# A second-layer loop with the quarter sums on another engine, one-bank accumulators and a second value buffer (Trainium2, one core)

## The chip, the cores and the metric

The kernel runs on one core of a Trainium2 chip. The metric is device time in microseconds (us): the median over several executions.

## The reference, cut to what matters

Attention feeds a gated layer, and that feeds a second layer. Only the second layer is touched by the change, apart from a few operations that are fitted into the end of the first.

```python
# attention: B=4, H=8, S=576, D=64, scores below max - tau are dropped -> x: 2304 tokens x 512
# layer 1: x1 = (sigmoid(x @ w_gate) * (x @ w_val)) @ w_out        (hidden 1536)
# layer 2: hidden 2048
h = x1 @ w_in
g = np.where(h >= 1, h, np.where(h <= -1, 0.0, (h + 1) ** 2 / 4.0))
return (g @ w_out).astype(np.float32)
```

## The kernel before, in words

**Numbers.** A float32 operand is held as a high part (rounded to fp32r) and a low part (value minus high part). Each product is three matmuls: high·high, high·low, low·high. ScalarE makes each high part by a copy, VectorE makes the low part by a subtraction.

**Stages.** Attention takes the time to about 290 us, layer 1 to about 747 us, layer 2 the rest. Layer 2 goes over the 2304 tokens in three passes of 768 (`NPASS`), and in each pass over 8 pairs of hidden blocks (`NQ`), 24 pairs in all, numbered from 0. Pairs 0, 8 and 16 are the first of a pass.

**A pair** (`pair`, L658). The up projection of a pair is a 2×2 block product done with seven products, P0 to P6 (`product`, L609), instead of eight. Each is six matmuls of 384 columns into one of two one-bank PSUM tiles `pu`. The token side of the seven products is built from sums and differences of the four quarters of the pass's input (two halves of the features, two halves of the tokens): `x_sums` (L565, four operations, L575 to L578) makes them once per pass, and `x_split` (L581: ScalarE L584, VectorE L585) splits seven blocks of them into high and low. The weight side is `tsum`, loaded per pair, and `w_split` (L587: ScalarE L591, VectorE L592) splits it: blocks of 512, 256 and 1024 columns.

Between the products small operations free the PSUM tiles and put the results together: after P0 ScalarE copies the tile to `s1` (L688); after P1 VectorE adds `c[0]`'s first token half (L677); after P2 ScalarE copies `u2` (L699); after P3, P4, P5, P6 VectorE adds again (all group under the line of the helper, L677). So P2 waits for the `s1` copy, P3 for the first add, P4 for `u2`, P5 and P6 for adds. The two results `c[0]` and `c[1]` (768 columns each) go through `activate` (L624): ScalarE does relu and square into `sqs` (L627, L628), VectorE a max and min (L630, here STT for its name SCALAR_TENSOR_TENSOR), ScalarE the high part `hh` (L631), VectorE the low part `hl` (L633). `out_split` (L598) splits the down weights `wout` (ScalarE L601, VectorE L602).

**The down projection** of a pair (`down_pair`, L715, matmul L723) is 36 matmuls of 512 columns into six accumulators of a PSUM bank each, held as three two-bank tiles `w`. It stands on TensorE behind the products of the next pair: products of pair q, down of pair q−1, products of pair q+1. It needs `hh`, `hl` and both `wout` parts of pair q−1. TensorE's order is fixed.

**Order of the other work.** Splits and the steps of `activate` are put on a list by `due`, with a date, a first and a last slot and a cost; `fill` (twice in a pair: behind P1, and at the pair's end) takes from it what fits the room. That sets the order in which ScalarE's and VectorE's in-order queues get their instructions. The SP queue issues the loads of a pair (`load_sums`, `load_pair`) and the stores of the pass before in one order.

**Ends of passes.** Layer 1's last token block is copied out of PSUM by `finish` (L746; VectorE L750, ScalarE L752), alternately. At the end of a pass `store` (L754, L764 and L766) copies the accumulators out the same way and stores them; this is behind the first down projection of the next pass. `x_sums(t + 1)` stands in pair 6 and 14 (j = NQ−2) in the code and runs on GpSimd, and `x_sums(0)` stands in layer 1's last steps. Behind the last pair, the tail does blocks 0 to 3 of `down_pair(22)` first, then interleaves the rest with the last pair's.

Of the kernel before, what the change touches and what calls it, by code (L numbers as in the profile page):

```python
# [10 lines left out]
F32 = mybir.dt.float32  # L11
# [18 lines left out]
def kernel(  # L30
# [17 lines left out]
    nc = tc.nc  # L48
# [23 lines left out]
    dram = ctx.enter_context(pool("dram", 2, space=DRAM))  # L72
    ps_w = ctx.enter_context(pool("ps_w", 1, space=PSUM))

# [124 lines left out]
    def attention():  # L199
# [4 lines left out]
        ps_o = ctx.enter_context(ExitStack())  # L204
        banks = ps_o.enter_context(pool("ps_o", 1, space=PSUM))
        left, av = (banks.tile([P, 512], F32, name=n) for n in ("left", "av"))
# [248 lines left out]
    def ffn(att):  # L455


        with ExitStack() as st:
# [108 lines left out]
            def x_sums(t):  # L567

                a11, a12, a21, a22 = (
                    xall[:, k * HK : (k + 1) * HK, t * T + n * HT :][:, :, :HT] for n in range(2) for k in range(2)  # L570
                )
                flat = [ssum[:, i] for i in range(2)]
                s1, s2, s4 = (x.rearrange("p (k t) -> p k t", k=HK) for x in (*flat, early_raw[0][:, : BX // 2]))
                op = nc.gpsimd.tensor_tensor
                op(s1, a21, a22, op=ALU.add)  # L575
                op(s2, s1, a11, op=ALU.subtract)
                op(s4, a12, s2, op=ALU.subtract)
                op(a21, a11, a21, op=ALU.subtract)  # L578
# [44 lines left out]

            def activate(i, c, h):  # L624

                r = sqs[:, i]
                nc.scalar.activation(r, c, AF.Relu, scale=0.5, bias=half)  # L627
                nc.scalar.activation(r, r, AF.Square)  # L628
                yield
                nc.vector.scalar_tensor_tensor(c, c, 1.0, r, op0=ALU.max, op1=ALU.min)  # L630
                nc.scalar.activation(h[0], c, AF.Copy)  # L631
                yield
                nc.vector.tensor_tensor(h[1], c, f32(h[0]), op=ALU.subtract)  # L633
                yield
# [7 lines left out]

            def due(at, release, last, cost, what):
                waiting.append((at, len(waiting), release, last, cost, what))
                waiting.sort(key=lambda x: x[:2])

            def fill(slot, room):
                while True:
                    now = [x for x in waiting if x[2] <= slot and (x[4] <= room or x[3] <= slot)]
                    if not now:  # L650
                        return
                    x = now[0]
                    waiting.remove(x)
                    room -= x[4]
                    x[5]()

            def due_x(t):
                q = t * NQ  # L658
                for i in range(7):
                    first = 3 * (q - 1) + max(1, min(i, 2))  # L660
                    last = 3 * q - 1 if i < 2 else 3 * q + 1
                    due(start(q) + i - 1, first, last, 0.93, lambda i=i: x_split(t, i))

            def due_w(q):
                for i, (p, first, last, cost) in enumerate(
                    ((0, 3 * q - 2, 3 * q - 1, 0.67), (6, 3 * q - 1, 3 * q + 1, 0.4), (2, 3 * q - 1, 3 * q + 1, 1.2))
                ):
                    due(start(q) + p - 1, first, last, cost, lambda i=i: w_split(q, i))

            def pair(q):  # L670

                t, j = divmod(q, NQ)
                ps = [ps_a.tile([P, 512], F32, tag=f"a{i}", name="pu")[:, :HT] for i in range(2)]
                c = [vals[:, 0], (vals[:, 1], rbs, early_raw[1])[q % 3][:, :T]]
                s1, u2 = (hp_.tile([P, HT], F32, tag="act", name="act") for _ in range(2))
# [15 lines left out]
                fill(3 * q + 1, 1.5)  # L691
# [38 lines left out]
            def at(y, a, b):  # L730
                return y[a // 1024].rearrange("p a b -> p (a b)")[:, a % 1024 : a % 1024 + b - a]

# [21 lines left out]
            def store(t, y, i):  # L754
                x = xall[:, :, t * T : (t + 1) * T]
                o = x[:, i, :DM].unsqueeze(1) if i < KD else x[:, 2 * (i - KD) : 2 * (i - KD) + 2, DM:]
                src = y[i % 3][:, i // 3].rearrange("p (a b) -> p a b", a=o.shape[1])
                r0 = t * T + i * P
# [55 lines left out]
            cp = cv("cp", 1, side="right")  # L814
            ps_a = sb("ps_a", 1, space=PSUM)
            for i in range(2):
# [10 lines left out]
            run(more, second)  # L827
            wides.extend(taken)
            NS = len(order)
            for s in range(NS):  # L830
# [5 lines left out]
                if s == NS - 3:  # L836
# [17 lines left out]
                if s == NS - 1:  # L854
# [3 lines left out]
                    due_w(0)  # L858
                    fill(-1, 4.4)
                _, t, f = order[s - 1]  # L860
                if s > 0:
                    if f == 0:
                        y = [wide() for _ in range(3)]
                    down(t, f, y)
                    if f == NF[0] - 1:
                        finish(t, y)
            for q in range(NPASS * NQ):
# [67 lines left out]
```

## Time and profile before

| | |
|---|---|
| median of 3 runs | 1162.38 us (1161.56 to 1163.65) |
| profiled execution, its own time | 1163.97 us |
| its span in the trace | 1161.9 us |
| mean granted TensorE clock, share of full | 0.988 |
| TensorE matmul busy | 1118.1 us, 96% of the span |
| VectorE busy | 848.2 us, 73% |
| ScalarE busy | 619.4 us, 53% |
| GpSimd busy | 166.5 us, 14% |

The profile's page comes from one execution. Engines are PE (TensorE matmul), PEld (its weight loads), DVE (VectorE), ACT (ScalarE), POOL (GpSimd) and SP (the queue that issues DMAs). A row of a timeline gives start, duration, engine, line, operation, output and inputs, shapes and count; in brackets stands how long the engine was idle before it, and what released it.

### The profile page before, as it was taken

What the parts mean: (1) busy time and instruction counts of PE and PEld (TensorE: products, weight loads), DVE (VectorE), ACT (ScalarE), POOL (GpSimd) and SP (SyncE); (2) the same over time, 40 slices, a digit from 0 to 9 for tenths busy, and PEclk for the clock granted to TensorE, in tenths of its full rate; (3) what the DMA queues carried; (4) which work ended last, traced back from release to release, by engine and by line L of the source; (5) the groups of instructions that cost most, each with busy time, mean ns of one, the idle gap of its engine ahead of it and who ended that gap; (6) DMA issues with size and microseconds to landing.
All of it is one profiled execution on the core that took longest, in us unless ns stands there. A gap on an engine that the chain in (4) does not pass through costs nothing.

```text
span 1161.9 us, 17313 instructions
## 1 busy us (share of the span) xinstructions
PE 1118.1 (96%) x6372; PEld 949.1 (82%) x6372; DVE 848.2 (73%) x1472; ACT 619.4 (53%) x1048; POOL 166.5 (14%) x327
## 2 busy tenths in 40 slices
PE   8999999999899999999999999989998999999998
PEld 5655655656799999999999999878987888878886
DVE  7888888887699998776786672656667666766663
ACT  5777777777444435333343322455565565655653
POOL 3444544454100000000000030110004000000000
PEclk9999999999899999999999999989998999999999
DMA  4323223222556555555455343122331433233301
GB/s 128 90 76 97 72 73 81 70 55 66 210 165 207 199 192 207 181 168 182 149 181 189 111 142 113 55 73 92 108 109 55 163 109 109 90 125 112 109 19 54
DMA packets 65140, 139.08 MB, mean 120 GB/s; under 512 B 9616, under 2 KB 35872, under 8 KB 65056
## 3 DMA queue, kind: packets, MB, share of 16 engines
q1 hardware_dynamic: 64912, 137.98, 35.9%
q8 instruction: 50, 0.82, 0.3%
q14 instruction: 34, 0.28, 0.1%
q10 hardware_dynamic: 144, 0.00, 0.0%
HBM read 111.15 MB, written 26.81 MB: 119 GB/s over the span
## 4 chain that ended last, share of the span: by engine, by line
PE 80%; DVE 11%; ACT 4%; issue 3%; DMA 1%; SPq 0%; POOL 0%; DVEq 0%; POOLq 0%; ACTq 0%
PE w L723 13%; PE pu L619 13%; PE w L741 12%; PE pgv L484 8%; PE pgv L485 8%; PE pgv L486 8%; PE av L318 6%; PE w L294 5%; PE w L251 5%; DVE s L260 2%; PE w L247 2%; DVE p L280 1%; DVE win L592 1%; DVE vals L630 1%; DVE high L164 1%
## 5 line engine op out<-in xcount | busy, mean ns | idle before, releaser
L484 PE MATMUL pgv<-xflat,win 128*128 128x384 f32 x560 | 189.1, 338 | 5.7 <-ACT act L540 4.1
L485 PE MATMUL pgv<-xflat,win 128*128 128x384 f32 x560 | 188.6, 337 | 0.1
L486 PE MATMUL pgv<-xflat,win 128*128 128x384 f32 x560 | 188.5, 337 | 0.0
L723 PE MATMUL w<-wout,hh 128*128 128x512 f32 x576 | 184.3, 394 | 0.6 <-ACT hh L631 0.6
L741 PE MATMUL w<-hh,wout 128*128 128x512 f32 (+1 forms) x576 | 147.2, 338 | 0.0
L260 DVE TENSOR_SCALAR_CACHE_REDUCE s<-w,nscale 128x576 f32<-128x576 f32 x144 | 112.7, 817 | 33.2 <-PE w L251 23.4
L723 PEld LDWEIGHTS w<-wout,hh 128*128 128x128 f32 x576 | 108.2, 188 | 25.4 <-ACT hh L631 1.1
L619 PE MATMUL pu<-xflat,win 128*128 128x384 f32 x576 | 112.8, 351 | 8.9 <-ACT act L699 4.8
L619 PEld LDWEIGHTS pu<-xflat,win 128*128 128x128 f32 x576 | 105.8, 198 | 12.5 <-ACT act L699 6.6
L723 PE MATMUL w<-wout,hl 128*128 128x512 f32 x288 | 113.7, 395 | 0.5 <-DVE hl L633 0.5
L484 PEld LDWEIGHTS pgv<-xflat,win 128*128 128x128 f32 x560 | 106.2, 190 | 8.5 <-ACT act L540 5.0
L280 DVE SCALAR_TENSOR_TENSOR p<-s,mx,ex 128x576 f32<-128x576 f32 x144 | 112.0, 811 | 0.5 <-POOL lt L287 0.5
L544 DVE TENSOR_TENSOR act<-pgv,act 128x384 f32<-128x384 f32 x70 | 38.9, 555 | 98.4 <-PE pgv L486 97.1
L272 ACT ACTIVATE ex<-s,mx 128x576 f32<-128x576 f32 x144 | 104.8, 775 | 6.5 <-DVE s L260 6.1
L741 PEld LDWEIGHTS w<-hh,wout 128*128 128x128 f32 x576 | 98.6, 189 | 11.4
L485 PEld LDWEIGHTS pgv<-xflat,win 128*128 128x128 f32 x560 | 106.2, 190 | 2.0 <-DVE xflat L476 0.4
L486 PEld LDWEIGHTS pgv<-xflat,win 128*128 128x128 f32 x560 | 106.1, 190 | 0.0
L540 ACT ACTIVATE act<-pgv 128x384 f32<-128x384 f32 x70 | 34.2, 489 | 133.3 <-PE pgv L486 133.1
L545 ACT ACTIVATE hh<-act 128x384 fp32r<-128x384 f32 x72 | 37.9, 526 | 119.7 <-DVE act L544 119.7
L741 PE MATMUL w<-hl,wout 128*128 128x512 f32 (+1 forms) x288 | 97.5, 338 | 0.0
L294 PEld LDWEIGHTS w<-ident,p 128*128 128x128 f32 x576 | 62.8, 141 | 41.6 <-ACT ex L272 36.6
L294 PE MATMUL w<-ident,p 128*128 128x128 f32 x576 | 79.4, 278 | 13.6 <-DVE p L280 10.5
(132 smaller groups left out, 1942.8 us busy)
## 6 DMA issues: line engine op xcount, KB each, us to landing
wmore<-saved SPq DMA_DIRECT2D x32, 512.0 KB
words<-in_moe_w_out_dram SPq DMA_DIRECT2D x26, 512.0 KB
tsum<-tsaved SPq DMA_DIRECT2D x24, 512.0 KB
wmore<-saved SPq DMA_DIRECT2D x15, 768.0 KB
words<-in_moe_w_in_dram SPq DMA_DIRECT2D x16, 512.0 KB
saved<-w SPq DMA_DIRECT2D x16, 512.0 KB
w<-saved SPq DMA_DIRECT2D x16, 512.0 KB
w<-saved SPq DMA_DIRECT2D x9, 768.0 KB
```

The costliest lines, as they stand in the source:

```text
L251: nc.tensor.matmul(w[:, s, :HS], t[es, 0, u * P : u * P + P], t[es, 1, c], start=True, stop=True)
L260: nc.vector.tensor_scalar(t[:, e], w[:, :, :HS], nscale, None, op0=ALU.mult, op1=ALU.min, accum_out=mx[:, 0, e : e + 1])
L272: nc.scalar.activation(ex[:, e], t[:, e], AF.Exp, scale=-1.0, bias=mx[:, 0, e : e + 1])
L280: nc.vector.scalar_tensor_tensor(pr[:, e], t[:, e].rearrange("p a b -> p (a b)"), mx[:, 1, e : e + 1], ex[:, e].rearrange("p a b -> p (a b ...
L294: nc.tensor.transpose(wt[:, e, cs], pr[:, e, cs], ident)
L318: nc.tensor.matmul(av[e * D : e * D + D, :n], vs[p % 3][:, e, c], rt[r][:, e, c] if c < nf else rl[r], start=c == 0, stop=c == nf,)
L484: nc.tensor.matmul(ps, ih[:, i, kk], xh[:, kk, c], start=(kk == 0), stop=False)
L485: nc.tensor.matmul(ps, ih[:, i, kk], xl[:, kk, c], start=False, stop=False)
L486: nc.tensor.matmul(ps, il[:, i, kk], xh[:, kk, c], start=False, stop=(kk == KD - 1))
L619: nc.tensor.matmul(ps[bank], l[:, k], r[:, k], start=bool(new) and k == m == 0, stop=k == HK - 1 and m == 2, skip_group_check=True,)
L723: nc.tensor.matmul(y[b % 3][:, b // 3], l[:, ts_], r, start=first and m == 0, stop=last and m == 2)
L741: nc.tensor.matmul(at(y, a, b), l[:, ds_], r[:, c], start=new and m == 0, stop=last and m == 2, skip_group_check=True,)
```

## The change

1. The four operations of `x_sums` move from GpSimd to VectorE. For the first pass they are worked into a step of layer 1. For the next passes they are put on the list in pair 4 (12), at dates from 8 units past the start of pair 5 (13) on, and `x_sums` in pair 6 (14) goes.
2. The six accumulators become six tiles `y_0` to `y_5` of one bank. `finish` gives even banks to VectorE and odd ones to ScalarE; before, it alternated piece by piece.
3. `c[0]` alternates between `sqs[:, 1]` and `vals[:, 0]`; before it was always `vals[:, 0]`. Both halves' squares go through the one buffer `sqs[:, 0]`; before, each had its own.
4. `due` and `fill` count ScalarE's time next to VectorE's, with other costs and other last slots.
5. In the tail the blocks 0 to 4 of `down_pair(22)` come first, and the last pair's second relu is dated earlier.

```diff
-                op = nc.gpsimd.tensor_tensor
+                op = nc.vector.tensor_tensor
                 op(s1, a21, a22, op=ALU.add)
+                yield
...
-            def activate(i, c, h):
-
-                r = sqs[:, i]
+            def activate(c, r, h):
+
                 nc.scalar.activation(r, c, AF.Relu, scale=0.5, bias=half)
...
-            def fill(slot, room):
+            def fill(slot, room, act):
                 while True:
-                    now = [x for x in waiting if x[2] <= slot and (x[4] <= room or x[3] <= slot)]
+                    now = [x for x in waiting if x[2] <= slot and (x[4] <= room and x[5] <= act or x[3] <= slot)]
...
                     room -= x[4]
-                    x[5]()
+                    act -= x[5]
+                    x[6]()
...
-                c = [vals[:, 0], (vals[:, 1], rbs, early_raw[1])[q % 3][:, :T]]
+                c = [(sqs[:, 1], vals[:, 0])[q % 2], (vals[:, 1], rbs, early_raw[1])[q % 3][:, :T]]
...
+                if j == NQ - 4 and t + 1 < NPASS:
+                    g = x_sums(t + 1)
+                    for i in range(4):
+                        due(start(q + 1) + 8 + 10 * i, 3 * q, 3 * (q + 3) - 1, 0.92, 0, lambda g=g: next(g))
...
-                    due(at - 1.8 + 0.3 * i, 3 * q, 3 * q + 2, 0.67, lambda i=i: out_split(q, i))
+                    due(at - 1.8 + 0.3 * i, 3 * q, 3 * q + 4, 0.6, 0.5, lambda i=i: out_split(q, i))
...
-                if j == NQ - 2 and t + 1 < NPASS:
-                    x_sums(t + 1)
...
-                    g = activate(i, c[i], h[i])
-                    for when, cost in (((-4, 0), (-1.9, 0.92), (-1.7, 0.92)), ((-1.6, 0), (1, 0.92), (2.5, 0.92)))[i]:
-                        last = 3 * q + 2 if i == 0 else 3 * q + 5
-                        due(at + when, 3 * q + 2, last, cost, lambda g=g: next(g))
-                fill(3 * q + 2, LEN(q) - (8 if j == 0 else 6))
+                    g = activate(c[i], vals[:, 1] if i and not more else sqs[:, 0], h[i])
+                    when = ((-4, -1.9, -1.7), (-1.6 if more else -3, 1, 2.5))[i]
+                    for w, d, a in zip(when, (0, 0.85, 0.85), (1.6, 0.72, 0)):
+                        due(at + w, 3 * q + 2, 3 * q + 5, d, a, lambda g=g: next(g))
+                drain = 2 if j == 0 else 0
+                fill(3 * q + 2, LEN(q) - 6 - drain, LEN(q) - 6 - drain)
...
-                                y[b % 3][:, b // 3], l[:, ts_], r, start=first and m == 0, stop=last and m == 2
+                                y[b], l[:, ts_], r, start=first and m == 0, stop=last and m == 2
...
-                    if i % 2 == 0:
+                    if a // 512 % 2 == 0:
                         nc.vector.tensor_copy(dst, at(y, a, b))
...
-                    x_sums(0)
+                    work = x_sums(0)
...
+                        yp = sb("ps_y", 1, space=PSUM)
+                        y = [yp.tile([P, 512], F32, name=f"y_{i}") for i in range(T // P)]
...
-            for b in (range(4), (4,), (5,)):
+            for b in (range(5), (5,)):
                 down_pair(q - 1, y, b)
```

TensorE's order is the same but for the tail, SP's is the same, and GpSimd loses its twelve sums. On ScalarE and VectorE the order moves at the starts and ends of passes and in pairs 4 and 12; in a regular pair it stays. Line numbers of the changed kernel are up to 9 higher.

ScalarE in pair 0, between the end of layer 1 and pair 1 (`xall<-w` and `xall<-y` are `finish`'s copies; `act<-pu` is `s1` or `u2`). Before:

```order
L631 ACTIVATE hh<-vals 128x768
L601 ACTIVATE wout_89<-wmore 128x512
L601 ACTIVATE wout_3013<-wmore 128x512
L752 ACTIVATE xall<-w_128 128x256
L752 ACTIVATE xall<-w_127 128x512
L752 ACTIVATE xall<-w_126 128x256
L752 ACTIVATE xall<-w_126 128x512
L688 ACTIVATE act<-pu 128x384
L627 ACTIVATE sqs<-vals,half 128x768
L628 ACTIVATE sqs<-sqs 128x768
L631 ACTIVATE hh<-vals 128x768
L699 ACTIVATE act<-pu 128x384
```

After:

```order
L760 ACTIVATE xall<-y_3229 128x256 x2
L760 ACTIVATE xall<-y_3231 128x512
L760 ACTIVATE xall<-y_3233 128x512
L697 ACTIVATE act<-pu 128x384
L606 ACTIVATE wout_89<-wmore 128x512
L635 ACTIVATE hh<-sqs 128x768
L606 ACTIVATE wout_3013<-wmore 128x512
L706 ACTIVATE act<-pu 128x384
```

The first pair's `hh` and both `wout` copies stood ahead of `finish`'s copies and of pair 1's `s1`; now they stand behind `s1`, and between it and `u2`. The second relu and square moved from ahead of `u2` to behind it.

ScalarE in pair 8, the first of the second pass. Before:

```order
L584 ACTIVATE xflat<-raw_86 128x768
L631 ACTIVATE hh<-vals 128x768
L601 ACTIVATE wout_6533<-wmore 128x512
L688 ACTIVATE act<-pu 128x384
L627 ACTIVATE sqs<-rb,half 128x768
L628 ACTIVATE sqs<-sqs 128x768
L631 ACTIVATE hh<-rb 128x768
L699 ACTIVATE act<-pu 128x384
L591 ACTIVATE win_88<-wmore 128x512
```

After:

```order
L589 ACTIVATE xflat<-raw_86 128x768
L635 ACTIVATE hh<-vals 128x768
L697 ACTIVATE act<-pu 128x384
L606 ACTIVATE wout_6543<-wmore 128x512
L706 ACTIVATE act<-pu 128x384
L631 ACTIVATE sqs<-rb,half 128x768
L632 ACTIVATE sqs<-sqs 128x768
L635 ACTIVATE hh<-rb 128x768
L596 ACTIVATE win_88<-wmore 128x512
```

The `u2` copy (the second `act<-pu`) moved ahead of the relu, square and `hh` of pair 7's second half.

VectorE at the end of pair 4 and the start of pair 5. Before:

```order
L630 SCALAR_TENSOR_TENSOR vals<-vals,sqs 128x768
L633 TENSOR_TENSOR hl<-vals,hh 128x768
L602 TENSOR_TENSOR wout_3013<-wmore,wout_3013 128x512
L630 SCALAR_TENSOR_TENSOR rb<-rb,sqs 128x768
L633 TENSOR_TENSOR hl<-rb,hh 128x768
L677 TENSOR_TENSOR vals<-pu,act 128x384
```

After:

```order
L634 SCALAR_TENSOR_TENSOR sqs<-sqs 128x768
L637 TENSOR_TENSOR hl<-sqs,hh 128x768
L607 TENSOR_TENSOR wout_3013<-wmore,wout_3013 128x512
L576 TENSOR_TENSOR ssum<-xall 128x768
L634 SCALAR_TENSOR_TENSOR rb<-rb,sqs 128x768
L637 TENSOR_TENSOR hl<-rb,hh 128x768
L578 TENSOR_TENSOR ssum<-ssum,xall 128x768
L580 TENSOR_TENSOR raw_86<-xall,ssum 128x768
L682 TENSOR_TENSOR vals<-pu,act 128x384
```

Three of the four sums stand in the pair's last stretch, two of them between the last `hl` and the add of pair 5 that P3 waits for; the fourth comes one pair later.

## Rows read from the trace of the kernel before

**Rows 1.** Page, part 1: busy time of the engines.
```profile
PE 1118.1 (96%) x6372; PEld 949.1 (82%) x6372; DVE 848.2 (73%) x1472; ACT 619.4 (53%) x1048; POOL 166.5 (14%) x327
```
**Rows 2.** Chain of waits (start, us, what): layer 1's last matmuls, first products of five pairs.
```profile
743.44 4.19 PE w L741 x24
...
802.89 7.33 PE pu L619 x42
...
865.63 7.34 PE pu L619 x42
...
938.55 7.33 PE pu L619 x42
...
1001.59 7.34 PE pu L619 x42
...
1069.41 7.33 PE pu L619 x42
```
**Rows 3.** Timeline of PE at the starts of the three passes.
```profile
755.08 3.13 PE L619 MATMUL pu<-xflat,win 128*128 128x384 f32 x12 [1.94 <-DVE high L677]
...
768.96 0.44 PE L619 MATMUL pu<-xmore,win 128*128 128x384 f32 x1 [3.66 <-ACT act L688]
...
887.28 1.32 PE L619 MATMUL pu<-xflat,win 128*128 128x384 f32 x6 [2.16 <-DVE vals L677]
...
890.59 0.69 PE L619 MATMUL pu<-xflat,win 128*128 128x384 f32 x1 [1.98 <-ACT act L699]
...
1023.71 0.62 PE L619 MATMUL pu<-xflat,win 128*128 128x384 f32 x2 [1.47 <-ACT act L699]
```
**Rows 4.** Windows: stretch, length, PE, PEld, DVE, ACT, POOL busy, granted clock, DMA share, GB/s.
```profile
755.00:766.00 11.00, 10.23 (x48) 9.22 (x48) 7.40 (x12) 4.95 (x8) 3.34 (x2) 0.84 0.25 70
770.00:777.00 7.00, 6.37 (x21) 5.86 (x20) 2.08 (x3) 2.51 (x5) 0.00 (x0) 0.51 0.00 0
873.00:885.00 12.00, 11.66 (x54) 9.52 (x52) 11.09 (x13) 8.45 (x13) 5.82 (x2) 1.00 0.24 87
891.00:897.00 6.00, 6.00 (x21) 5.91 (x21) 1.60 (x4) 2.51 (x4) 0.00 (x0) 0.55 0.00 0
1020.00:1024.00 4.00, 2.53 (x14) 2.04 (x14) 2.14 (x4) 2.94 (x5) 0.00 (x0) 1.00 0.40 131
```
**Rows 5.** Timeline of VectorE in pair 8.
```profile
884.46 2.31 DVE L602 TENSOR_TENSOR wout<-wmore,wout 128x512 fp32r<-128x512 f32 x1
...
887.15 2.13 DVE L630 SCALAR_TENSOR_TENSOR rb<-rb,sqs 128x768 f32<-128x768 f32 x1
```
**Rows 6.** Timeline of GpSimd in pair 8.
```profile
883.79 2.42 POOL L576 TENSOR_TENSOR ssum<-ssum,xall 128x768 f32<-128x768 f32 x1
```
**Rows 7.** Timeline of VectorE around the start of pair 7, a regular pair.
```profile
863.68 0.69 DVE L602 TENSOR_TENSOR wout<-wmore,wout 128x512 fp32r<-128x512 f32 x1 [1.27 <-ACT wout L601]
864.29 0.95 DVE L630 SCALAR_TENSOR_TENSOR vals<-vals,sqs 128x768 f32<-128x768 f32 x1
...
867.82 0.56 DVE L677 TENSOR_TENSOR vals<-pu,act 128x384 f32<-128x384 f32 x1 [0.70 <-PE pu L619]
```
**Rows 8.** ScalarE's groups, 930 to 1000 us, by form: busy, mean ns, idle before, releaser.
```profile
L628 ACT ACTIVATE sqs<-sqs 128x768 f32<-128x768 f32 x10 | 8.5, 848 | 0.3
L627 ACT ACTIVATE sqs<-vals,half 128x768 f32<-128x768 f32 x6 | 5.5, 920 | 0.0
L591 ACT ACTIVATE win<-tsum 128x1024 fp32r<-128x1024 f32 x5 | 5.3, 1062 | 12.8 <-PE pu L619 12.8
L631 ACT ACTIVATE hh<-vals 128x768 fp32r<-128x768 f32 x6 | 5.1, 847 | 8.4 <-DVE vals L630 8.4
L601 ACT ACTIVATE wout<-wmore 128x512 fp32r<-128x512 f32 x5 | 3.1, 614 | 0.0
...
L688 ACT ACTIVATE act<-pu 128x384 f32<-128x384 f32 x4 | 2.0, 492 | 2.6 <-PE pu L619 2.6
```
**Rows 9.** Page, part 5: a group of the down projection's matmuls.
```profile
L723 PE MATMUL w<-wout,hh 128*128 128x512 f32 x576 | 184.3, 394 | 0.6 <-ACT hh L631 0.6
```

More of the change, by code (lines that the diff above doesn't have):

```diff
@@ L72 @@
     dram = ctx.enter_context(pool("dram", 2, space=DRAM))
-    ps_w = ctx.enter_context(pool("ps_w", 1, space=PSUM))
+    ps_st = ctx.enter_context(ExitStack())
+    ps_w = ps_st.enter_context(pool("ps_w", 1, space=PSUM))
     ident = const.tile([P, P], F32, name="ident")
@@ L204, in attention @@
         ps_o = ctx.enter_context(ExitStack())
-        banks = ps_o.enter_context(pool("ps_o", 1, space=PSUM))
+        banks = ps_o.enter_context(pool("ps_o", 1, space=PSUM, side="right"))
         left, av = (banks.tile([P, 512], F32, name=n) for n in ("left", "av"))
@@ L573, in x_sums @@
                 s1, s2, s4 = (x.rearrange("p (k t) -> p k t", k=HK) for x in (*flat, early_raw[0][:, : BX // 2]))
-                op = nc.gpsimd.tensor_tensor
+                op = nc.vector.tensor_tensor
                 op(s1, a21, a22, op=ALU.add)
+                yield
                 op(s2, s1, a11, op=ALU.subtract)
+                yield
                 op(s4, a12, s2, op=ALU.subtract)
+                yield
                 op(a21, a11, a21, op=ALU.subtract)
                 xops[t] = (a11, a12, s2, a21, s1, a22, s4)
+                yield
             def x_split(t, i):
@@ L641, in ffn, with due @@
             start = lambda q: sum(LEN(i) for i in range(q))
-            def due(at, release, last, cost, what):
-                waiting.append((at, len(waiting), release, last, cost, what))
+            def due(at, release, last, cost, act, what):
+                waiting.append((at, len(waiting), release, last, cost, act, what))
                 waiting.sort(key=lambda x: x[:2])
-            def fill(slot, room):
+            def fill(slot, room, act):
                 while True:
-                    now = [x for x in waiting if x[2] <= slot and (x[4] <= room or x[3] <= slot)]
+                    now = [x for x in waiting if x[2] <= slot and (x[4] <= room and x[5] <= act or x[3] <= slot)]
                     if not now:
@@ L661, in due_x @@
                     last = 3 * q - 1 if i < 2 else 3 * q + 1
-                    due(start(q) + i - 1, first, last, 0.93, lambda i=i: x_split(t, i))
+                    due(start(q) + i - 1, first, last, 0.92, 0.72, lambda i=i: x_split(t, i))
             def due_w(q):
                 for i, (p, first, last, cost) in enumerate(
-                    ((0, 3 * q - 2, 3 * q - 1, 0.67), (6, 3 * q - 1, 3 * q + 1, 0.4), (2, 3 * q - 1, 3 * q + 1, 1.2))
+                    ((0, 3 * q - 2, 3 * q - 1, 0.6), (6, 3 * q - 1, 3 * q + 1, 0.3), (2, 3 * q - 1, 3 * q + 1, 1.1))
                 ):
-                    due(start(q) + p - 1, first, last, cost, lambda i=i: w_split(q, i))
+                    due(start(q) + p - 1, first, last, cost, cost - 0.1, lambda i=i: w_split(q, i))
             def pair(q):
@@ L690, in pair @@
                 add(c[0][:, t0], ps[1], s1)
-                fill(3 * q + 1, 1.5)
+                fill(3 * q + 1, 1.5, 1.3)
                 if more:
@@ L730, in at @@
             def at(y, a, b):
-                return y[a // 1024].rearrange("p a b -> p (a b)")[:, a % 1024 : a % 1024 + b - a]
+                return y[a // 512][:, a % 512 : a % 512 + b - a]
             def down(t, f, y):
@@ L756, in store @@
                 o = x[:, i, :DM].unsqueeze(1) if i < KD else x[:, 2 * (i - KD) : 2 * (i - KD) + 2, DM:]
-                src = y[i % 3][:, i // 3].rearrange("p (a b) -> p a b", a=o.shape[1])
+                src = y[i].rearrange("p (a b) -> p a b", a=o.shape[1])
                 r0 = t * T + i * P
@@ L814, in ffn @@
             cp = cv("cp", 1, side="right")
-            ps_a = sb("ps_a", 1, space=PSUM)
+            ps_a = sb("ps_a", 1, space=PSUM, side="right")
             for i in range(2):
@@ L827, in ffn @@
             run(more, second)
-            wides.extend(taken)
             NS = len(order)
@@ L858, in ffn @@
                     due_w(0)
-                    fill(-1, 4.4)
+                    fill(-1, 4.4, 4.4)
                 _, t, f = order[s - 1]
                 if s > 0:
-                    if f == 0:
-                        y = [wide() for _ in range(3)]
+                    if s == 1:
+                        ps_st.close()
+                        yp = sb("ps_y", 1, space=PSUM)
+                        y = [yp.tile([P, 512], F32, name=f"y_{i}") for i in range(T // P)]
                     down(t, f, y)
@@ L872, in ffn @@
                 elif q < NPASS * NQ - 1:
-                    if (q - 1) % NQ == 0:
-                        y = [wide() for _ in range(3)]
                     down_pair(q - 1, y)
```

## The prediction, made before the changed kernel ran

> **What bounds the kernel now.** I read the page first: TensorE's matmuls fill 96% of the span, VectorE 73%, ScalarE 53% [rows 1]. So other engines cost something only where they make TensorE wait or where its clock is low; a saving elsewhere is worth nothing by itself.
>
> Next the chain of waits, for what a pair costs and where pairs cost more. From pair 3's start at 802.89 to pair 7's at 865.63 are four pairs: 62.74 us, 15.685 each, of which 7.33 are the seven products and 8.36 the down projection [rows 2]. Against that scale:
>
> - Start of pass 0: layer 1's matmuls end at 743.44 + 4.19 = 747.63. Until pair 3 starts TensorE has three times 7.33, once more 4.19 (layer 1's last block) and twice 8.36: 42.9 us. It took 55.26. Lost: 12.4.
> - First boundary: pair 7 to pair 11 took 72.92, against 62.74. Lost: 10.2.
> - Second boundary: pair 15 to pair 19 took 67.82. Lost: 5.1.
>
> Some 28 us, then, lie where the change moves things. TensorE's timeline shows the waits: 1.94 and 3.66 us in the first stretch, 2.16 and 1.98 in the second, one of 1.47 in the third; the rest are below a microsecond each [rows 3]. The windows show the rest of the loss: the granted clock was 0.84 in 755 to 766, 0.51 in 770 to 777 and 0.55 in 891 to 897, between full (2.4 GHz) and half (1.2 GHz), and 1.00 behind the 1.47 wait [rows 4]. At 0.84 for 11 us 1.8 us of work are lost, at 0.51 for 7 us 3.4, at 0.55 for 6 us 2.7.
>
> Then why VectorE is late at the first boundary and less so at the second. In pair 8 one low part of `wout` takes 2.31 us and one STT 2.13 [rows 5]; in a regular pair they take 0.69 and 0.95 [rows 7]. In that stretch GpSimd runs the sums for the pass after (one of them from 883.79 for 2.42 us [rows 6]). The second boundary has no sums to run and lost 5.1 us less. I take GpSimd's sums as the cause of the slow VectorE.
>
> **The change part by part.** All sums are against the profiled execution, 1163.97 us; it is 1.6 above the median of the runs shown.
>
> *Sums off GpSimd, and the new list, start of pass 0.* The 1.94 wait (released by VectorE) goes with the contention. The 3.66 wait is for `s1`, behind `hh`, two `wout` copies and four copies of `finish`; these now stand behind it or run with one-bank tiles that ScalarE and VectorE empty side by side. That wait goes too. What comes late next is `u2` of pair 1: ScalarE now has two `wout` copies and `hh` between `s1` and `u2`. From P1's end the chain is add 0.56, `wout` low 0.69, STT 0.95 [rows 7], `hh` 0.85, `wout` 0.61, `u2` 0.49 [rows 8]: 4.15, while TensorE has P2 and P3, 2.1 (7.33/7 each): some 2.05, and 1.8 with a little overlap of the links. Behind `u2` stand relu 0.92, square 0.85, STT 0.95, `hh` 0.85 and an `hl` of about 0.95: 4.5, against three products, 3.1: the down projection waits 1.2. In pair 2 add, STT, `hh`, a 512-column copy and `u2` make 3.5 against 2.1: 1.05 after overlap. With 0.55 of small waits the stretch loses 4.6 in place of 12.4: **−7.8**. Ends: none of the new waits (−12.4), and all of them with nothing overlapped and a clock fall of 3.4 (−3.5).
>
> *First boundary.* `u2` now comes ahead of relu, square and `hh` of pair 7's second half, and VectorE runs at its regular speed: the two waits of 2.16 and 1.98 go. In pair 9 `s1` is late: from pair 8's last add (865.63 + 15.69 + 7.33 + 0.56 = 889.2) the queues hold STT, `hh`, a 512-column copy, the `tsum` copy 1.06, relu, square, 256 columns on each engine (0.4 each, by the slope from 614 to 1062 ns [rows 8]), STT, `hh`, `wout`, relu, square, three copies of 512 columns and `s1`: 12.6, about 11.4 with 0.07 or so of overlap at each link. That is 900.6; P2 could start at 865.63 + 31.37 + 2.1 = 899.1. It waits 1.5; P4 then waits 1.2 for `u2` by the same kind of chain, and pair 10 some 0.7 for a `tsum` load behind the stores. Loss 3.4 in place of 10.2: **−6.8**. *Second boundary*, same order, no sums before either: 3.4 in place of 5.1: **−1.7**. Ends for each: no wait at all, and the old loss unchanged (0).
>
> *Sums on VectorE in pairs 4 and 12.* Of the four operations three stand ahead of the add that P3 of pair 5 (13) waits for. No row shows them; the nearest are the STT and low parts of the same size, 0.95. Three make 2.85. In front of the add VectorE has idled 0.70, and 1.27 earlier in waiting for ScalarE [rows 7], of which some 0.7 can take the first sum. So P3 waits 1.45, twice: **+2.9**. Ends: 0 (all in idle time) and 4.3 (only the 0.70 helps). The fourth operation, a pair later, lies in the slack. GpSimd's other work is untouched, and `x_sums(0)` lies in layer 1, where TensorE is covered.
>
> *Second value buffer, one square buffer.* In the regular pair the second relu stands behind the first `hh`, which already waits for the STT that frees the square buffer; so it costs 0 there; a rival below has the other case. *Tail.* `hh` is dated earlier and one more block of work lies ahead of it: the 0.6 wait [rows 9] goes: **−0.6** (0 to −1.6 with small waits beside it). DMA: the issue order of SP is the same and the bytes too; costs 0.
>
> **Sum:** −7.8 −6.8 −1.7 +2.9 −0.6 = −14.0. 1163.97 − 14.0 = 1150.0 against the profile's own time; 1148.4 against the median.
>
> A page speaks against this change. The Trainium skill ("Perfetto Trace Analysis", section "Optimizing Scalar/DVE Operations") names GpSimd as a place for work when VectorE is saturated, and this change goes the other way: VectorE is busy 11.09 of 12 us in 873 to 885 [rows 4]. The same section warns that the two engines share a read port, and rows 5 against rows 7 agree with the warning.
>
> **The rivals.**
>
> *The clock falls at the new waits.* Before, it was low behind 1.94 and behind 2.16 with 1.98, and not behind 1.47 [rows 3, 4]; the new waits of 1.8, 1.5 and 1.2 lie around that. A fall costs 1.8 to 3.4 us [rows 4]. One to three falls give 1150.2 to 1158.6, about 1153.6 with two. For it: pairs of waits stand close together in pairs 1 and 9. Against it: each alone is shorter than those that cost clock. The Trainium skill ("TensorE: Matmul & The Clock Gate", section "Why this matters for your kernels") warns only of idle stretches longer than any wait in my sum; by that rule this rival would be nothing and the time 1148.4, and the trace does not agree, since the clock fell in 755 to 766 behind 1.94.
>
> *The mid-pass waits don't come* (the first end above): 1148.4 − 2.9 = 1145.5; for it that VectorE waits for ScalarE several times in a pair's second half.
>
> *GpSimd is not the cause*, and the slow VectorE operations come from something that stays, the traffic in that stretch say. Then 5.1 at the first boundary and 1.94 at the start stay: a gain of 7.0, 1155.4. Against it: all long operations that I saw stand where GpSimd runs, and the second boundary has none.
>
> *Slower: the one square buffer ties the halves together.* If the second relu got ahead of the first half's `hh` in a regular pair, ScalarE would stand still until VectorE's STT has read the first square. Place: ScalarE's queue in some 21 regular pairs; price: up to the 1.40 us that ScalarE idles for that STT (8.4 us in 6 [rows 8]). 21 × 1.40 = 29.4 us would give 1177.8; from 14.0/21 = 0.67 us a pair the gain is gone. Against it: in the listed order of regular pairs the second relu stands behind that `hh`.
>
> **How the numbers follow.** The forecast has 0.58, the clock 0.20, no mid-pass waits 0.08, GpSimd not the cause 0.08, the square buffer 0.06. The likeliest case gives **1148.4**. The range takes in the ends of the mid-pass price below and the clock's cases above: **1143 to 1157**, which leaves out the square buffer, the upper end of the clock, and the unlikely ends of the boundary terms. A measurement of this kernel can tell about 0.2% (2.3 us) from no change. Faster by more: all but the square buffer and a part of GpSimd's case, 0.90; within: 0.04; slower: 0.06.
>
> **What would show it.** Right: regular VectorE durations (0.69 and 0.95) in pairs 0 and 8; TensorE's idle before pair 3 down to about 5 us; pair 7 to 11 and pair 15 to 19 alike at some 66 us; a wait of 1 to 2 us before P3 in pairs 5 and 13, released by VectorE's add; granted clock 1.00 through both boundaries. A regular pair stays at 15.685. Wrong: a clock below 0.9 behind the new waits; regular pairs above 15.7; VectorE's operations still at 2 us; or pair 8's loss merely moved into pair 9 at its old size.

## The result, and the profile after

On the same chip the changed kernel takes 1152.0 us (median of 4 runs, 1151.8 to 1152.6), the kernel before 1162.0 (1160.6 to 1163.7): ratio 0.9914, 95% interval 0.9897 to 0.9932. That is 10 us faster; 14 were forecast, and the range of 1143 to 1157 holds it. The profiled executions stand at 1163.97 and 1151.81, 12.2 apart; the first is above all timed runs of its kernel.

The chain of waits of the changed kernel (start, us, what), for the pairs that answer to [rows 2]: the first products of pairs 0, 3, 7, 11, 15 and 19, and the tail.

```profile
746.78 7.38 PE pu L624 x42
...
794.90 7.58 PE pu L624 x42
...
859.75 7.32 PE pu L624 x42
...
927.15 7.32 PE pu L624 x42
...
991.76 7.35 PE pu L624 x42
...
1058.80 7.32 PE pu L624 x42
...
1128.90 16.78 PE y L731 x72
```

Differences of these starts, beside those of before, give a table by stage (us). The runs of the next section are in it too, by the same view of their own traces; "end" is the last matmul. A row's stages come from one execution, the profiled one, its ratio from all: the profiled one of e1 stands 2.5 us above the median of its runs, that of e3 2.2 below, that of the kernel before 2.0 above, the others closer.

| kernel | ratio (95%) | pair 0–3 | 3–7 | 7–11 | 11–15 | 15–19 | 19–end |
|---|---|---|---|---|---|---|---|
| before | 1 | 55.3 | 62.7 | 72.9 | 63.1 | 67.8 | 88.6 |
| changed | 0.9914 (0.9897–0.9932) | 48.1 | 64.9 | 67.4 | 64.6 | 67.0 | 87.0 |
| e1 | 0.9949 (0.9933–0.9966) | 52.1 | 63.1 | 70.3 | 63.1 | 67.2 | 87.1 |
| e2 | 0.9950 (0.9937–0.9963) | 50.4 | 64.7 | 67.7 | 64.7 | 67.9 | 88.7 |
| e3 | 0.9886 (0.9873–0.9899) | 48.1 | 63.1 | 66.9 | 62.8 | 66.9 | 87.1 |
| e4 | 0.9966 (0.9954–0.9978) | 49.9 | 62.7 | 72.9 | 63.1 | 67.5 | 88.7 |
| e5 | 0.9927 (0.9912–0.9942) | 48.1 | 64.9 | 67.5 | 64.6 | 66.9 | 88.6 |
| e6 | 0.9936 (0.9923–0.9948) | 48.5 | 66.7 | 66.9 | 66.7 | 66.8 | 87.0 |
| e7 | 0.9916 (0.9903–0.9930) | 47.2 | 64.7 | 68.2 | 64.6 | 67.2 | 88.7 |
| e8 | 0.9852 (0.9835–0.9869) | 48.2 | 63.0 | 65.5 | 62.8 | 65.4 | 87.0 |
| e9 | 0.9915 (0.9901–0.9928) | 52.7 | 63.0 | 67.6 | 62.7 | 67.7 | 87.0 |
| e10 | 0.9872 (0.9857–0.9886) | 50.9 | 63.1 | 65.6 | 62.8 | 65.7 | 87.0 |
| e11 | 0.9874 (0.9857–0.9890) | 51.9 | 62.8 | 65.7 | 62.8 | 65.7 | 87.1 |
| e12 | 0.9851 (0.9835–0.9868) | 49.0 | 62.8 | 65.4 | 62.8 | 65.4 | 87.0 |

From pair 0 to the end the change gains 7.1 + 5.5 + 0.8 + 1.5 and loses 2.1 + 1.5: 11.3 us. TensorE's timeline of the changed kernel has these waits, in place of those of [rows 3]:

```profile
764.38 0.81 PE L624 MATMUL pu<-xflat,win 128*128 128x384 f32 x3 [1.87 <-ACT act L706]
...
769.32 0.50 PE L731 MATMUL y<-wout,hl 128*128 128x512 f32 x1 [1.28 <-DVE hl L637]
...
783.20 0.97 PE L624 MATMUL pu<-xflat,win 128*128 128x384 f32 x4 [0.96 <-ACT act L706]
...
831.26 0.97 PE L624 MATMUL pu<-xflat,win 128*128 128x384 f32 x4 [1.58 <-DVE vals L682]
...
895.04 1.14 PE L624 MATMUL pu<-xmore,win 128*128 128x384 f32 x5 [1.75 <-ACT act L697]
...
1027.09 1.14 PE L624 MATMUL pu<-xmore,win 128*128 128x384 f32 x5 [1.75 <-ACT act L697]
...
1030.46 0.79 PE L624 MATMUL pu<-xflat,win 128*128 128x384 f32 x3 [1.02 <-ACT act L706]
```

Added up, waits of over 0.3 us from the start of pass 0 on fell from 17.3 to 12.8 us. VectorE is back at its regular durations in pair 8, where [rows 5] had 2.31 and 2.13:

```profile
889.08 0.95 DVE L634 SCALAR_TENSOR_TENSOR sqs<-sqs 128x768 f32<-128x768 f32 x1
891.47 0.69 DVE L607 TENSOR_TENSOR wout<-w,wout 128x512 fp32r<-128x512 f32 x1 [1.43 <-ACT wout L606]
```

Most of the rest came back from the clock. The windows of the changed kernel (columns as in [rows 4]):

```profile
755.00:765.00 10.00, 8.13 (x47) 7.41 (x46) 6.72 (x12) 6.28 (x12) 0.00 (x0) 1.00 0.32 105
771.00:777.00 6.00, 6.00 (x27) 4.82 (x26) 3.99 (x5) 4.61 (x8) 0.00 (x0) 1.00 0.27 87
896.00:900.00 4.00, 3.82 (x15) 3.31 (x14) 1.66 (x3) 1.74 (x3) 0.00 (x0) 0.57 1.05 356
1025.00:1031.00 6.00, 3.23 (x17) 2.59 (x17) 4.51 (x8) 4.30 (x9) 0.00 (x0) 1.00 0.81 276
```

In [rows 4] low clock cost 1.8 + 3.4 + 2.7 us; here one fall is left, 0.43 × 4 = 1.7. So of the 11.3 us between these two executions some 4.5 are idle time won and some 6 are clock.

### The profile page after: what moved, and what is told of

Its sections match the earlier page's. It is cut to its first block, busy times and chain, and to the rows that moved or that the text cites. A ratio compares the mean times of both kernels' runs of the same rounds, so it can differ in the third digit from the quotient of the medians.

```text
span 1150.0 us, 17327 instructions
## 1 busy us (share of the span) xinstructions
PE 1110.5 (97%) x6372; PEld 943.8 (82%) x6372; DVE 845.8 (74%) x1484; ACT 618.8 (54%) x1048; POOL 138.4 (12%) x315
## 4 chain that ended last, share of the span: by engine, by line
PE 83%; DVE 9%; ACT 5%; issue 3%; DMA 0%; SPq 0%; DVEq 0%; ACTq 0%
PE y L731 14%; PE pu L624 14%; PE y L749 13%; PE pgv L486 8%; PE pgv L485 8%; PE pgv L487 8%; PE av L319 6%; PE w L295 5%; PE w L252 5%; DVE s L261 2%; PE w L248 2%; DVE p L281 1%; ACT hh L635 1%; ACT sqs L631 1%; DVE high L165 1%
## 5 line engine op out<-in xcount | busy, mean ns | idle before, releaser
L731 PE MATMUL y<-wout,hh 128*128 128x512 f32 x576 | 184.1, 394 | 0.0
L749 PE MATMUL y<-hh,wout 128*128 128x512 f32 (+1 forms) x576 | 146.5, 336 | 0.0
L731 PEld LDWEIGHTS y<-wout,hh 128*128 128x128 f32 x576 | 108.2, 188 | 24.4
L731 PE MATMUL y<-wout,hl 128*128 128x512 f32 x288 | 113.7, 395 | 1.3 <-DVE hl L637 1.3
L624 PE MATMUL pu<-xflat,win 128*128 128x384 f32 x576 | 107.4, 340 | 7.2 <-ACT act L706 4.0
L624 PEld LDWEIGHTS pu<-xflat,win 128*128 128x128 f32 x576 | 101.5, 190 | 9.7 <-ACT act L706 5.5
L749 PEld LDWEIGHTS y<-hh,wout 128*128 128x128 f32 x576 | 98.0, 188 | 11.3
L749 PE MATMUL y<-hl,wout 128*128 128x512 f32 (+1 forms) x288 | 97.1, 337 | 0.0
L295 PEld LDWEIGHTS w<-ident,p 128*128 128x128 f32 x576 | 62.8, 141 | 41.6 <-ACT ex L273 36.6
```

Of the source, the lines that this page charges most:

```text
L295: nc.tensor.transpose(wt[:, e, cs], pr[:, e, cs], ident)
L624: nc.tensor.matmul(ps[bank], l[:, k], r[:, k], start=bool(new) and k == m == 0, stop=k == HK - 1 and m == 2, skip_group_check=True,)
L731: nc.tensor.matmul(y[b], l[:, ts_], r, start=first and m == 0, stop=last and m == 2)
L749: nc.tensor.matmul(at(y, a, b), l[:, ds_], r[:, c], start=new and m == 0, stop=last and m == 2, skip_group_check=True,)
```

## The experiments

**Where the sums run: e1 and e2.** e1 is the changed kernel with the sums back on GpSimd, e2 the kernel before with the sums alone on VectorE.

```diff
 # e1, from the changed kernel; e2 makes the opposite edit in the kernel before
-                op = nc.vector.tensor_tensor
+                op = nc.gpsimd.tensor_tensor
...
-                if j == NQ - 4 and t + 1 < NPASS:
-                    g = x_sums(t + 1)
...
+                if j == NQ - 2 and t + 1 < NPASS:
+                    x_sums(t + 1)
```

> The changed kernel (1152.0) with the quarter sums back on GpSimd, called where the kernel before calls them; all else as changed. Theory G (GpSimd's sums slow VectorE's operations at the starts of passes 0 and 1): the pairs 3 to 7 and 11 to 15 go back from 64.9 and 64.6 us to about 62.8 (3.7 us won), the first boundary (pair 7 to pair 11) rises from 67.4 by 4 to 6 us, the start of pass 0 (48.1 us) by 1.5 to 4: 1153.8 to 1158.3 in all. Theory O (the new order on the list did it, the engine of the sums does not matter there): the boundary stays at 67.4 and the start at 48.1, only the mid-pass waits go: 1148.3.

Measured: 0.9949 against 0.9914, 4 us slower than the changed kernel. The mid-pass waits went (63.1 and 63.1), the first boundary rose by 2.9, less than the 4 to 6 expected. The start rose by 4.0; a wait of 1.90 us came back there, with a granted clock of 0.72 in 757 to 763. So theory O falls. This execution also reached pair 0 3.8 us later than the changed kernel, which the table leaves out; e6, which has the first pass's sums at the same place, reached it 0.9 earlier.

> The kernel before (1162.0) with the sums alone moved to VectorE; they land at the same places of VectorE's queue in pairs 4, 5, 12 and 13 as in the changed kernel. Theory G: the 1.94 us wait at the start of pass 0 goes (with or without 1.8 us of clock), the first boundary falls from 72.9 to the second's 67.8, the mid-pass waits cost 3.7: 1157.0 to 1158.8. Theory O: no gain at the starts, the mid-pass waits come: 1165.7.

Measured: 0.9950, 1156.6 us, 0.4 below the lower end of what theory G gave. The first boundary is 67.7, equal to the second's 67.9 as expected; the start won 4.8, though its 3.66 wait became 4.48. VectorE and GpSimd of e1 in pair 8 show the mechanism:

```profile
884.13 2.44 DVE L633 TENSOR_TENSOR hl<-vals,hh 128x768 fp32r<-128x768 f32 x1
886.49 2.29 DVE L603 TENSOR_TENSOR wout<-wmore,wout 128x512 fp32r<-128x512 f32 x1
888.71 0.55 DVE L678 TENSOR_TENSOR high<-pu,act 128x384 f32<-128x384 f32 x1
```
```profile
883.89 1.87 POOL L577 TENSOR_TENSOR ssum<-ssum,xall 128x768 f32<-128x768 f32 x1
885.83 2.41 POOL L578 TENSOR_TENSOR raw<-xall,ssum 128x768 f32<-128x768 f32 x1
888.20 2.28 POOL L579 TENSOR_TENSOR xall<-xall 128x768 f32<-128x768 f32 x1
```

The `hl` that takes 0.96 elsewhere takes 2.44 and ends (884.13 + 2.44) 0.8 us behind the GpSimd operation beside it (883.89 + 1.87); the `wout` part, 0.69 elsewhere, ends 0.5 behind the next. TensorE then waits 2.52 us for the add at 888.71:

```profile
889.31 0.97 PE L620 MATMUL pu<-xflat,win 128*128 128x384 f32 x4 [2.52 <-DVE high L678]
```

**The banks and the list: e4 and e7.** e4 is the kernel before with the one-bank accumulators alone, e7 with these and the sums on VectorE; old list, old tail, one value buffer.

```diff
...
-                                y[b % 3][:, b // 3], l[:, ts_], r, start=first and m == 0, stop=last and m == 2
+                                y[b], l[:, ts_], r, start=first and m == 0, stop=last and m == 2
...
-                    if i % 2 == 0:
+                    if a // 512 % 2 == 0:
                         nc.vector.tensor_copy(dst, at(y, a, b))
...
```

> The kernel before with the one-bank accumulators alone (and finish's even banks on VectorE, odd on ScalarE). Theory B (the tiles let ScalarE and VectorE empty the last block side by side): the 3.66 us wait at the start of pass 0 falls by 1 to 2.5 us, boundaries and regular pairs stay: 1159.5 to 1161. Rival L (the order of the list alone removes that wait): no change, 1162, the 3.66 wait stays within 0.3.

Measured: 0.9966, 4 us faster, more than theory B gave. At the start of pass 0 the 3.66 wait is 1.41 (but two of 0.8 follow), and the clock stayed up, which B had not counted:

```profile
755.00:770.00 15.00, 11.99 (x64) 10.50 (x65) 10.76 (x17) 10.24 (x17) 3.20 (x2) 1.00 0.33 105
```

> The kernel before with two parts of the change, the sums on VectorE and the one-bank accumulators; old list, old tail, one value buffer. Theory P (the list and the second value buffer bring little beside the tail): start of pass 0 at 47 to 49.5, first boundary 67.7, second 67.7, mid-pass and tail as in e2: 1153 to 1154.5, within 2.5 of the changed kernel, of which the tail is 1.5. Rival D (the new list is needed for the start): the start stays at 50 or more, 1156 and above.

Measured: 0.9916, the same as the whole change, as theory P had it. The start is 47.2, a microsecond better than with the new list, the boundaries 68.2 and 67.2.

**The tail: e5.**

```diff
-                    when = ((-4, -1.9, -1.7), (-1.6 if more else -3, 1, 2.5))[i]
+                    when = ((-4, -1.9, -1.7), (-1.6, 1, 2.5))[i]
...
-            for b in (range(5), (5,)):
+            for b in (range(4), (4,), (5,)):
```

> The changed kernel with the tail of before (blocks 0 to 3 of the down projection before last first, second relu of the last pair at its old date). Theory T (the 1.5 us won behind pair 19 come from these two lines alone): pair 19 to the end goes back from 87.0 to 88.6, with waits of 0.6 for hh and 0.5 for hl in the tail; all other stretches as in the changed kernel; 1153.5. Rival: the one-bank tiles or the order of the last pairs' splits won it, the stretch stays at 87.0.

Measured: 0.9927, 1154.0; 88.6 us behind pair 19, waits of 0.66 and 0.49, the rest unchanged. The two lines are worth about 1.5 us. e5 and e7 differ in the list and the value buffers alone, and their intervals overlap (0.9927 and 0.9916): these two parts of the change win nothing that the runs can tell.

**Where the sums stand: e3 and e6.** e3 keeps them on VectorE, two per pair, at dates between STT and `hl` and between `hl` and the `wout` low part. e6 keeps them on GpSimd and holds them back to pair 4 (12).

```diff
 # e3, from the changed kernel
-                    for i in range(4):
-                        due(start(q + 1) + 8 + 10 * i, 3 * q, 3 * (q + 3) - 1, 0.92, 0, lambda g=g: next(g))
+                    for d in (-1.85, -1.65):
+                        due(start(q + 1) + 7 + d, 3 * q + 2, 3 * q + 2, 0, 0, lambda g=sums[t + 1]: next(g))
...
 # e6, from e1
+                if j == NQ - 4 and t + 1 < NPASS:
+                    nc.gpsimd.tensor_tensor(ssum[:, 0, :1], u2[:, :1], u2[:, :1], op=ALU.add)
+                    x_sums(t + 1)
```

> The changed kernel with the sums at other places of VectorE's queue: one between STT and the first hl (where VectorE idles 0.91 us for hh), one between that hl and the wout low part (idle 1.27), in each of pairs 4, 5, 12 and 13. Theory S (the place in the queue costs the waits, not the work): both 1.58 us waits and the 0.5 after each go, 1148.3, pairs 3 to 7 take 62.8. Rival W (VectorE has no room in a pair for more work, what is moved comes back as another wait): the time stays at 1152.

Measured: 0.9886, 1149.7; no wait over 0.3 us is left in pairs 4, 5, 12 and 13, so theory S holds. VectorE in the changed kernel, and then in e3:

```profile
827.92 0.96 DVE L637 TENSOR_TENSOR hl<-rb,hh 128x768 fp32r<-128x768 f32 x1 [0.91 <-ACT hh L635]
828.80 0.95 DVE L578 TENSOR_TENSOR ssum<-ssum,xall 128x768 f32<-128x768 f32 x1
829.78 0.96 DVE L580 TENSOR_TENSOR raw<-xall,ssum 128x768 f32<-128x768 f32 x1
830.66 0.55 DVE L682 TENSOR_TENSOR vals<-pu,act 128x384 f32<-128x384 f32 x1
```
```profile
821.38 0.96 DVE L576 TENSOR_TENSOR ssum<-xall 128x768 f32<-128x768 f32 x1
822.38 0.96 DVE L637 TENSOR_TENSOR hl<-sqs,hh 128x768 fp32r<-128x768 f32 x1
823.26 0.95 DVE L578 TENSOR_TENSOR ssum<-ssum,xall 128x768 f32<-128x768 f32 x1
...
828.76 0.56 DVE L682 TENSOR_TENSOR vals<-pu,act 128x384 f32<-128x384 f32 x1 [0.73 <-PE pu L624]
```

In the changed kernel two sums stand straight ahead of the add. In e3 the first takes just the time in which VectorE would wait for `hh`, and the add waits for TensorE again.

> Run e1 (sums on GpSimd) with the sums held back to pair 4 (12): a GpSimd operation of one column that reads u2 of that pair stands ahead of them. All else as e1. Theory G: GpSimd's sums lengthen VectorE's operations wherever they meet them. In pair 4 they run from the third product on for about 8 us and the adds and low parts there go from 0.56 and 0.95 to 1 to 2.3 us; TensorE waits 2 to 5 us in pairs 4 and 5, the pairs 3 to 7 take 65 to 68, those of 11 to 15 alike, and the start of pass 0 and the first boundary fall to what the changed kernel has (48.1 without a clock fall, 67.4): 1151 to 1159. Rival F (GpSimd is free in mid-pass, only the crowded starts suffer): pairs 3 to 7 stay at 62.8 and the time is 1148 to 1149.

Measured: 0.9936; pairs 3 to 7 and 11 to 15 at 66.7, as theory G has it, with a wait of 1.9 in each and a clock fall behind it. But the adds did not get longer: those beside GpSimd's first two sums took 0.56. VectorE, and then GpSimd, in pair 4:

```profile
817.71 0.56 DVE L678 TENSOR_TENSOR rb<-pu,act 128x384 f32<-128x384 f32 x1 [0.48 <-PE pu L620]
818.19 1.22 DVE L593 TENSOR_TENSOR win<-tsum,win 128x1024 fp32r<-128x1024 f32 x1
819.60 1.81 DVE L593 TENSOR_TENSOR win<-w,win 128x256 fp32r<-128x256 f32 x1 [0.19 <-ACT win L592]
821.33 2.60 DVE L630 SCALAR_TENSOR_TENSOR sqs<-sqs 128x768 f32<-128x768 f32 x1
```
```profile
816.39 1.88 POOL L577 TENSOR_TENSOR ssum<-ssum,xall 128x768 f32<-128x768 f32 x1
818.35 2.77 POOL L578 TENSOR_TENSOR raw<-xall,ssum 128x768 f32<-128x768 f32 x1
821.08 2.04 POOL L579 TENSOR_TENSOR xall<-xall 128x768 f32<-128x768 f32 x1
```

So it is not an add that makes TensorE wait. The slow low part and STT delay the chain of `hh` and `hl` behind them, and `s1` of pair 5 stands at its end on ScalarE; P2 waits for it. TensorE, and the window behind:

```profile
829.94 1.54 PE L620 MATMUL pu<-xmore,win 128*128 128x384 f32 x5 [1.87 <-ACT act L689]
```
```profile
830.00:834.00 4.00, 4.00 (x14) 4.00 (x15) 2.35 (x5) 1.42 (x3) 0.00 (x0) 0.57 0.13 52
```

**Better starts: e8 to e12**, all on top of e3. e8 moves the copies and stores of the pass before into the products of pair 9 (17).

```diff
-                    if q % NQ == 0:
-                        for i in range(T // P):
-                            store(q // NQ - 1, y, i)
...
+                late = range(T // P) if j == 1 and t > 0 else ()
                 product(2, ps)
                 nc.scalar.activation(u2, ps[0], AF.Copy)
+                for i in late[1::2]:
+                    store(t - 1, y, i)
                 product(3, ps)
                 add(u3, ps[1], u2)
+                for i in late[:1]:
+                    store(t - 1, y, i)
...
```

> Run e3 with the copies and stores of the pass before moved from the end of pair 8 (16) into the products of pair 9 (17): ScalarE's three behind u2, VectorE's one behind each of three adds. Theory C (the 1.76 wait of pair 9 for s1 is the three copies ahead of it): that wait falls to 0.2 to 0.6, the one behind it for u2 (1.0) rises to 1.3 or so, both boundaries fall from 66.9 to 65.5 to 66.3: e3 less 1 to 3. Rival X (ScalarE and VectorE are full there, the copies come back as later waits): boundaries stay at 66.9 or rise.

Measured: 0.9852, 1144.9 us, the fastest median, 4 less than e3 by the ratios. The wait for `s1` is gone, the one for `u2` stayed at 1.0, and both boundaries are 65.4 to 65.5. Theory C holds.

e9, e10, e11 and e12 reorder the first and second pair of a pass.

```diff
 # e9, from e8: filling of pairs 1, 9, 17 behind the add after P3
+                if j == 1:
+                    fill(3 * q + 1, 1.5, 1.3)
 # e10, from e8: the filling, then the loads, right behind the u2 copy
                 nc.scalar.activation(u2, ps[0], AF.Copy)
+                if j == 1:
+                    fill(3 * q + 1, 1.5, 1.3)
+                    loads(q)
 # e11, from e10
-                fill(3 * q + 2, LEN(q) - 6 - drain, LEN(q) - 6 - drain)
+                fill(3 * q + 2, LEN(q) - 6 - drain, 99 if q == 0 else LEN(q) - 6 - drain)
 # e12, from e8: the same line, and for pair 0 out_split's last slot 2 and a cost of 0.2 for the second relu
```

> Run e8 with, in pairs 1, 9 and 17, the mid-pair filling moved from ahead of the u2 copy to behind the add after P3, so that u2 no longer waits behind wout and hh. Theory C: the waits for u2 go (1.9 in pair 1, 1.0 to 1.3 in pairs 9 and 17), P5 or P6 wait 0.3 to 1 for adds behind the filled-in work instead; start of pass 0 falls from 48.1 by 0 to 1.5, boundaries to 64 to 65.5: e8 less 1 to 3. Rival X: the chain of hh and hl for the down projection gets later by as much, the wait moves to it, and nothing is won.

> Run e8 with the mid-pair filling of pairs 1, 9 and 17 (and the loads behind it) moved from ahead of the u2 copy to right behind it: ScalarE takes s1, u2, then wout and hh; VectorE's order is as in e8. Run e9 had the filling behind the add after P3 and the loads ahead of it, so that its wout splits in these pairs read weights of a later load. Theory C (e9 lost because VectorE's STT and wout low part stood between the adds, and its wout split waited for a load): here the waits for u2 go (1.9 in pair 1, 1.0 in 9 and 17), P5 waits 0 to 0.7 for the add after P3; boundaries from 65.45 to 64.5 to 65.2, start of pass 0 from 48.1 to 47 to 48: 1 to 3 less than e8. Rival X (what is moved comes back, as in e9): boundaries at 65.4 or more, time as e8 or above.

> Run e10 with ScalarE's time not counted in the filling of pair 0, so that hh of its first half, and relu and square of its second, stand ahead of finish's copies, nearer to the old list. Theory N (the new list's count of ScalarE's time makes the start of pass 0 about 1 us longer: 48.1 in the changed kernel against 47.2 in e7): the hl wait of 1.28 goes, P2 of pair 1 waits 1 or so for s1; start of pass 0 at 46 to 47.5. Rival: relu and square ahead of the copies make s1 late by 2.5 and the start becomes 49 or more.

> Run e8 with the start of pass 0 put back near to the old list: pair 0's hh and both wout copies ahead of finish's copies, the second relu and square behind u2 of pair 1. Runs e10 and e11 have shown that shifting work behind or ahead of u2 there moves the wait (3.2 and 1.8 with 3.2). Theory N (the wout copies belong ahead of finish's copies, as in e7, 47.2): P2 of pair 1 waits about 1.1 for s1, P4 not at all, the hl wait falls below 0.7; start of pass 0 at 46 to 47.3, e8 (0.9852 of before) less 1 to 2 us. Rival X (the start holds a fixed amount of ScalarE and VectorE work, any order waits 4 us in all): 48 or more, e8's time or above.

Measured: e9 0.9915, e10 0.9872, e11 0.9874, e12 0.9851, so e12 equals e8, while e10 and e11 are some 2 us slower (their intervals touch e8's; the start of pass 0 is longer by 2.7 and 3.7), and e9 is clearly slower. e9 is no clean test: its loads stand ahead of the filling, so its `wout` splits in pairs 1, 9 and 17 read weights of a later load, and it does not compute this layer. Its time is given only for where its waits stand. The waits moved, as the rivals had it. In e9 P6 waits 2.68 in pair 1; in e10 P5 waits 3.17; in e11 pair 2 waits 3.17 for `s1`; in e12 pair 2 waits 2.65. TensorE of e10 in pair 1, and its window:

```profile
766.39 1.01 PE L624 MATMUL pu<-xflat,win 128*128 128x384 f32 x2 [3.17 <-DVE high L688]
```
```profile
766.00:770.00 4.00, 3.61 (x12) 3.61 (x13) 1.45 (x3) 0.84 (x1) 0.00 (x0) 0.57 0.38 131
```

In none of the orders tried does TensorE wait less than 3.1 us in all at the start of pass 0 (over 0.3 us each); whether a better one exists was not settled. Part of what these orders lose is clock: it was 0.50 in 768 to 777 of e9 and 0.58 in 782 to 786 of e12, and in e8 it stayed at 1.00 from 755 to 795. In e12 the waits at the start add up to 3.8 us against 4.1 in e8, and yet its start is 0.8 longer.

## Why the prediction was right, and where its sizes were off

**GpSimd's sums slow VectorE, and moving them wins the most.** Right, and shown both ways: e2 wins 5.8 us by that alone, e1 gives 4 back. The Trainium skill ("SBUF — State Buffer", section "Who interferes with whom") says that a VectorE instruction with two inputs in SBUF contends with a GpSimd instruction that reads SBUF, that one with at most one SBUF input does not (outside certain modes), and that the later of the two stands still. The trace of e6 agrees in all three: the add from PSUM keeps its 0.56, the low part and STT from SBUF go to 1.81 and 2.60 and end 0.3 and 0.8 us behind GpSimd's operations, and GpSimd's sum that began 0.16 us behind VectorE's 1.22 took 2.77 in place of 1.88.

**Start of pass 0, −7.8 forecast, −7.1 measured.** The new waits of 1.8, 1.2 and 1.05 came as 1.87, 1.28 and 0.96, in the places named. What the step put together was wrong in one part: the list did not help. e4 has 49.9 with the banks alone, e7 47.2 with banks and sums, the changed kernel 48.1 with the new list and the second value buffer on top. And where the step counted the end of old waits, over half of what came back was clock: 5.2 us in [rows 4], none here.

**First boundary, −6.8 forecast, −5.5 measured; second, −1.7 and −0.8.** The waits of pair 9 were put at 1.5 and 1.2 and came as 1.75 and 0.2; those of pair 17 as 1.75 and 1.02. The 0.7 for a `tsum` load in pairs 10 and 18 came as waits of 0.43 and 0.56, for `s1`. Behind the first 1.75 the clock fell, at 1.7 us by the window: the rival on the clock, once instead of the two falls that it was priced at. The step credited the place of `u2` and the regular speed of VectorE together; e2 and e7 have the old list and 67.7 and 68.2 against 67.4, so the sums alone did nearly all of it. The second boundary, where the forecast left the list alone to win, fell by 0.8 for 1.7; e7, with the old list, has 67.2 there against 67.0, so little of that is the list's either. The rest, 0.6 and 1.0 us of the 4.7 and 4.3 lost, is waits under 0.3 us and matmuls a little longer than in the steady pair, which the sum did not count.

**Mid-pass, +2.9 forecast, +3.7 measured.** The step was right in place and kind (P3 waits for the add, 1.58 in place of 1.45). Beside the wait pair 3's products take 7.58 us instead of 7.33, some 0.3 us that e3 shows too, without the sums in the way.

**Tail, −0.6 forecast, −1.5 measured**: mis-sized; e5 shows both waits and the small ones beside them, the far end of the given bound.

**The square buffer** costs nothing: regular pairs stay at 15.7 (e3, pairs 11 to 15: 62.8/4). The slower rival did not come, and "GpSimd is not the cause" fell with e1.

The sum of the terms thus missed 2.7 us of 14.0 (11.3 came). The profile that it was worked from stood 2 us above the median of that chip's runs, which makes the measured 10. Of the signs that the prediction named, those of being right came, the boundaries at 67 for 66, but for the clock: it was to stay at 1.00 through both boundaries, and the 0.57 behind the wait of pair 9 is one of its signs of being wrong.

## What to carry to other kernels

Before moving small work to an idle engine, look whether the operations that run beside it get longer; here eight GpSimd sums (four for each of two passes) cost more through VectorE than the same sums on VectorE itself. Once on the busy engine, their place in its queue decides: in the gaps where it waits for another engine they cost nothing, ahead of what TensorE waits for they cost 1.6 us each time. At a full start reordering moves waits about; taking work out of the crowded stretch (the stores of e8) removed the longest wait of each boundary.

## What the runs showed of the hardware that was not expected

The granted clock does not follow from the length of a wait alone (1.00 is 2.4 GHz; 0.57 over 4 us is most of them at half, 1.2 GHz). Behind the 1.75 wait at 893.3 it was 0.57 in 896 to 900, and behind the same 1.75, followed by 1.02, at 1025.3 it stayed at 1.00, in one execution. Behind the 1.94 at the start of pass 0 it fell in the kernel before and not in e4, which has the same wait. In e6 it was 0.57 behind the 1.87 of pair 5, and behind the 1.87 of pair 1 in the changed kernel it was 1.00 (755 to 765 and 765 to 771). The window that the prediction read for the 1.47 ends 0.3 us behind that wait; in 1024 to 1028 the clock was 1.00 too.

What a fall costs in the end differs as well. In e6 it comes in full: pairs 3 to 7 take 3.9 us more than the 62.7 of before, the wait of 1.87 and 1.7 of clock among them. In pair 9 of the changed kernel the slower products hid most of the next wait:

```profile
898.41 1.01 PE L624 MATMUL pu<-xflat,win 128*128 128x384 f32 x2 [0.18 <-ACT act L706]
```

That wait is 1.02 in pair 17, where the clock stayed up (1.01 in pair 9 of e3), and the first boundary is only 0.4 us longer than the second. So the same wait of 1.75 us can come with 1.7 us of lost clock or without, and how much of that reached the total differed with the wait behind it. What decides whether the clock falls was not tried. The Trainium skill ("TensorE: Matmul & The Clock Gate", section "Why this matters for your kernels") warns only of longer stretches of idle time; the runs go against that.
